# Joins and bank copies at the head of each half step of a fused FFT mixer and MLP; steps 0 and 1 side by side; table casts in stage A

## The chip, the cores and the metric

One Trainium2 chip, one core. The time is device microseconds of one launch. The kernel before has a median of 2609.62 us over 3 runs (2607.21 to 2612.15).

## The reference

For each of 8 sequences of 3008 tokens with 256 channels the reference takes a real FFT along the tokens, mixes the channels with a complex 256 x 256 matrix and a bias, applies a soft threshold of 0.01 to real and imaginary parts, and transforms back. All 24064 tokens then go through an MLP with a squared ReLU:

```python
X = np.fft.rfft(x, axis=1)
Yr = Xr @ w_r - Xi @ w_i + b_r
Yi = Xr @ w_i + Xi @ w_r + b_i
Yr = np.sign(Yr) * np.maximum(np.abs(Yr) - lam, 0.0)   # Yi likewise
y = np.fft.irfft(Y, n=x.shape[1], axis=1)
h = np.maximum(x @ w_in, 0.0)                          # w_in 256 x 2048
out = h * h @ w_out                                    # w_out 2048 x 256
```

## The kernel before

**Numbers.** Every large product is done in three matmuls (`mm3`), of a rounded high half and the low half that is left of both operands: high by high, high by low, low by high. So each tensor that TensorE (PE) reads is first split: ScalarE (ACT) casts the high half, VectorE (DVE) subtracts to get the low half.

**The transform.** 3008 = 47 x 64. Stage A transforms over 47 points, stage B over 64, then come the mix, the threshold, stage C (64 points back) and stage D (47 points back). A and B, and C and D, hand their data over through DRAM scratch. Two frequencies make a pair; there are 12 pairs for each sequence (batch). `start()` does stages A to D of batch 0 and stage A of batch 1, splits the weights that are needed first, then casts the tables of the mix (`tables_main`) and prepares the first chunk. All that uses a pool of memory of its own (`sb0`), which is given back before the main loop.

**The main loop.** The tokens are cut into 32 chunks of 752 columns. For each chunk the MLP has 8 steps (`u`), each for 256 of the 2048 hidden columns. Each step has two half steps (`r = 2u + h`, even and odd), and 516 half steps are written out in order. The first layer of a step is done with seven products (0 to 6, line 1010, a Winograd scheme over 2 x 2 blocks), three matmuls of 376 columns each. Products 0, 6, 5 and 1 add up in one PSUM bank x, which ACT copies out after each of them (lines 1127, 1142, 1157; the last with ReLU, line 1174); products 2, 4 and 3 use the other bank y, and DVE joins each to what the copies left (`join`, line 1017). The next product in a bank must wait until the copy or join of the one before it has read it. The results are squared on ACT (line 1108), split into gh (ACT, line 1113) and gl (DVE, `low`, line 1119), and two steps later (`LAG`) the second layer takes them: `mm2`, 12 matmuls in each half step, which are handed out in portions (`take_some`) between the products.

PE's order in an even half step is: product 0, product 3 of the step before, place p1, 6 of mm2, product 6, 3 of mm2, product 2, the other 3 of mm2, place p2. In an odd one: product 5, 3 of mm2, product 4, p1, 3 of mm2, product 1, the other 6 of mm2, p2.

**Transform work in the loop.** Batches 1 to 7 are transformed between the MLP's work. A planner puts each piece into a half step and a place there: `load` (DMA issues on SP, at the head), `p1` and `p2` (matmuls), `e`, `e2` and `f`, `f2` (what ACT and DVE do at once with a bank that p1 or p2 filled), and `a` (ACT) and `v` (DVE) for the rest that has no bank to empty. The rest of a pair is: xl on DVE in half step r; the threshold on DVE in r + 2; `turned` in r + 3, four ACT instructions (lines 880 and 881) that turn the thresholded halves round; zh on ACT and zl on DVE in r + 4. Stage A has fold, fh and fl there. The pairs of batch 1 stand 3 half steps apart, from r = 7 on, those of batch 2 stand 4 apart and those of batches 3 to 7 stand 5 apart (`pair_rounds`). Five tables of w_out are loaded late, one at a time into one buffer (`et`), and narrowed and split in places `a` and `v` (`plan_w`).

In the kernel before, `a` and `v` of a half step are the last thing in it. So on ACT they stand before the first bank copy of the next half step, and on DVE before `low` and, in an even half step, before join 3, which `low` precedes as well. Each engine does its instructions in the order in which they are written; waits between engines are semaphores.

The lines that the rows name: 198 to 200 are the three matmuls of `mm3`, 1025 those of mm2, 300 the low half of a chunk's operands (xa, xb, xc), 297 their high half, 856 is xl, 193 the low half of a table, 604 a copy in the first inverse, 334 the first instruction of narrowing.

Of the kernel before, what the change touches and what calls it, by code (L numbers as in the profile page):

```python
# [10 lines left out]
F32 = mybir.dt.float32  # L11
F32R = mybir.dt.float32r
U32 = mybir.dt.uint32
AF = mybir.ActivationFunctionType
ALU = mybir.AluOpType

P = 128
# [120 lines left out]
HALF = CH // 2  # L138


def crossed(x):

    return x.rearrange("p (a i) -> p i a", a=2)
# [21 lines left out]
def fft_mix_moe(ctx: ExitStack, tc: tile.TileContext, xp, xu, w_ri, b_ri,  # L165
                w_in, w_out, t_u, t_a, t_b, t_b0, t_m, t_d, sgn, outT):
    nc = tc.nc
# [22 lines left out]
    def split(src, hi, lo, engine=nc.vector):  # L190

        nc.scalar.copy(hi, src)
        engine.tensor_sub(lo, src, hi.bitcast(F32))
# [150 lines left out]
    def start():  # L344

        with ExitStack() as own:
# [82 lines left out]
            def tables_main():  # L429

                for k in range(2):
                    split(ms[:, 3 * k:3 * k + 3], wm[0][:, :, k], wm[1][:, :, k])
                    yield
                split(tM, tMs[:, 0], tMs[:, 1])
                yield
# [54 lines left out]
            def weights(begin=True):  # L490

                for p in list(going):
                    if next(p, going) is going:
                        going.remove(p)
                p = next(pending, None) if begin else None
                if p is not None:
                    next(p)
                    going.append(p)
                return bool(going)
# [89 lines left out]
            first = [i for i in range(len(flat)) if begins[i] < CH]  # L589
# [84 lines left out]
            late = table_a()  # L674
# [43 lines left out]
            inv = inverse()  # L718
            next(inv)
            nc.sync.dma_start(out=bias2.rearrange("p c e -> p (c e)"), in_=b_ri[0].partition_broadcast(P))  # L720
            for n, _ in enumerate(a1):
                for k in range(WE[n]):
                    weights()
            busy = x1[nq - 1][:NU1].rearrange("p k d -> p (k d)")
            for _ in range(WARM2):
                idle()
# [1 line left out]
                weights()  # L728
            for _ in inv:
                pass  # L730
            late = tables_main()
            while weights():
                next(late, None)
            for _ in late:
                pass

# [6 lines left out]
    ps_h = ctx.enter_context(tc.tile_pool(name="ps_h", bufs=1, space=bass.MemoryType.PSUM))  # L743
    ps_o = ctx.enter_context(tc.tile_pool(name="ps_o", bufs=1, space=bass.MemoryType.PSUM))
# [7 lines left out]
    def opnd(name, dt, bufs):  # L752
        return tl(name, (P, 2, HALF), dt, bufs=bufs)

    for tag, shape, dt, bufs in (("g0", (P, 2, HALF), F32, 2), ("g1", (P, 2, HALF), F32, 2),
                                 ("gh", (P, 2, HALF), F32R, 3), ("gl", (P, 2, HALF), F32R, 3), ("o", (P, 4, HALF), F32, 1),
                                 ("gap1", (P, 16), F32, 1), ("xh", (P, 3, 2, P), F32R, 1), ("xl", (P, 3, 2, P), F32R, 1),
                                 ("gap2", (P, 24), F32, 1), ("fh", (P, 512), F32R, 1), ("fl", (P, 512), F32R, 1),
                                 ("gap3", (P, 16), F32, 1), ("zh", (P, 2, D), F32R, 1), ("zl", (P, 2, D), F32R, 1)):
        tl(tag, shape, dt, bufs)  # L760
# [13 lines left out]
    def run(r, place):  # L774
        for do in plan.pop((r, place), ()):
            do()
# [232 lines left out]
    def product(s, u, bank, start=False):  # L1009
        c, j = divmod(u, NU)  # L1010
        name, n = XOP[s]
        w, x = wi_[j], xs_[c][name]
        mm3(bank[:, :HALF], (w[:, 0, s], w[:, 1, s]), (crossed(x[:, 0, n]), crossed(x[:, 1, n])), start, True,
            skip_group_check=True)

    def join(bank, g):
        nc.vector._custom_dve(TENSOR_ADD_SAT, out=g, in0=bank[:, :HALF], in1=g, s0=float("inf"), s1=0.0)  # L1017
# [58 lines left out]
        plan_w(j, r)  # L1076

    gs, cast, split_, pos, outs, stores = {}, {}, {}, {}, {}, []
    h0 = h1 = None

    def take_some(gen, n):
        for _ in range(n):
# [3 lines left out]
    with tc.manual_schedule():  # L1086
        for r in range(2 * (last + LAG)):
            u, h = divmod(r, 2)
            c, j = divmod(u, NU)
            k = u - LAG  # L1090
            cc, jj = divmod(k, NU)
            live, behind = u < last, 0 <= u - 1 < last
            nextx = live and c + 1 < nch and r % PER == PER - 1
            ends = k >= 0 and jj == NU - 1
            run(r, "load")
            while stores:
                stores.pop()()
            if k >= 0:
                if jj == 0:
                    pos[cc, h] = [ps_o.tile([P, 512], F32, tag=f"o{e}{h}", name="po") for e in range(2)]  # L1100
                second = mm2(jj, h, pos[cc, h], *split_.pop((k, h)))
            else:
                second = iter(())

            def squares():
                if behind:
                    g = gs[u - 1][h]
                    nc.scalar.activation(g, g, AF.Square)  # L1108

            def high():  # L1110
                if behind:
                    cast[u - 1, h] = opnd("gh", F32R, 3)
                    nc.scalar.copy(cast[u - 1, h], gs[u - 1][h])  # L1113

            def low():
                q = (u - 1, 0) if h else (u - 2, 1)
                if q in cast:
                    gh, gl = cast.pop(q), opnd("gl", F32R, 3)
                    nc.vector.tensor_sub(gl, gs[q[0]][q[1]], gh.bitcast(F32))  # L1119
                    split_[q] = gh, gl  # L1120

            if h == 0:
                if live:
                    gs[u] = [opnd(f"g{n}", F32, 2) for n in range(2)]
                    old, h0 = h1, ps_h.tile([P, 512], F32, tag="x", name="h0")
                    product(0, u, h0, True)
                    nc.scalar.copy(gs[u][0][:, 0], h0[:, :HALF])  # L1127
                else:
                    old = h1
                if behind:  # L1130
                    product(3, u - 1, old)
                low()
                if behind:
                    join(old, gs[u - 1][1][:, 0])
                run(r, "p1")
                run(r, "e")
                run(r, "e2")
                squares()
                take_some(second, 6)
                if live:  # L1140
                    product(6, u, h0)
                    nc.scalar.copy(gs[u][1][:, 0], h0[:, :HALF])  # L1142
                take_some(second, 3)
                if live:
                    h1 = ps_h.tile([P, 512], F32, tag="y", name="h1")
                    product(2, u, h1, True)
                    join(h1, gs[u][0][:, 0])
                if live and c and j == 0:
                    xc, x = new_x(c, "xc"), halves(raw_of(c))[:, 1:4:2]
                    high_x(xc, x, 0, 2)  # L1150
                    low_x(xc, x, 0, 2)
                high()
                take_some(second, 12)
            else:
                if live:
                    product(5, u, h0)
                    nc.scalar.copy(gs[u][1][:, 1], h0[:, :HALF])  # L1157
                low()
                take_some(second, 3)
                if live:  # L1160
                    product(4, u, h1, True)
                    join(h1, gs[u][1][:, 1])
                run(r, "p1")
                run(r, "e")
                run(r, "e2")
                if nextx:
                    xa, x = new_x(c + 1, "xa"), halves(raw_of(c + 1))[:, 0:3:2]
                    high_x(xa, x, 0, 2)
                    low_x(xa, x, 0, 2)
                squares()  # L1170
                take_some(second, 3)
                if live:
                    product(1, u, h0)
                    nc.scalar.activation(gs[u][0][:, 1], h0[:, :HALF], AF.Relu)
                if nextx:
                    xb = new_x(c + 1, "xb")
                    high_x(xb, ts[:, 0:3], 0, 3)
                    low_x(xb, ts[:, 0:3], 0, 3)
                high()
                take_some(second, 12)  # L1180
            run(r, "p2")
            rest = out(cc, h, pos.pop((cc, h))) if ends else iter(())
            next(rest, None)
            run(r, "f")
            run(r, "f2")
            next(rest, None)
            run(r, "a")
            run(r, "v")
            if live and c + 1 < nch and r % PER == PER - 3:
                ts = tl("o", (P, 4, HALF), name="ts")  # L1190
                diffs(c + 1, ts[:, 0:2], ts[:, 2])
        assert not stores
# [46 lines left out]
```

## Time and profile before

| | |
|---|---|
| median of 3 runs | 2609.62 us |
| the profiled execution's own time | 2608.95 us |
| its span | 2607.0 us |
| PE busy, matmuls / weight loads | 2467.1 us (95%) / 2339.3 us (90%) |
| ACT busy | 1859.0 us (71%) |
| DVE busy | 1653.1 us (63%) |
| mean granted TensorE clock | 0.993 |
| HBM traffic | 62 GB/s over the span |

The span runs from the first to the last instruction of the program. An engine's busy time is the union of its instructions' times. Matmuls overlap each other in the pipeline, so PE's busy time says less on holes than that of its weight loads (PEld), of which one stands before each matmul. In a row of the waits, the instruction on the left sat idle until the one on the right was done.

### The profile page before, as it was taken

What the parts mean: (1) busy time and instruction counts of PE and PEld (TensorE: products, weight loads), DVE (VectorE), ACT (ScalarE), POOL (GpSimd) and SP (SyncE); (2) the same over time, 40 slices, a digit from 0 to 9 for tenths busy, and PEclk for the clock granted to TensorE, in tenths of its full rate; (3) what the DMA queues carried; (4) which work ended last, traced back from release to release, by engine and by line L of the source; (5) the groups of instructions that cost most, each with busy time, mean ns of one, the idle gap of its engine ahead of it and who ended that gap; (6) DMA issues with size and microseconds to landing.
All of it is one profiled execution on the core that took longest, in us unless ns stands there. A gap on an engine that the chain in (4) does not pass through costs nothing.

```text
span 2607.0 us, 40095 instructions
## 1 busy us (share of the span) xinstructions
PE 2467.1 (95%) x15630; PEld 2339.3 (90%) x15630; DVE 1653.1 (63%) x2715; ACT 1859.0 (71%) x3332; POOL 26.1 (1%) x41
## 2 busy tenths in 40 slices
PE   9888899999999999999999999999999999999999
PEld 5478889999999889998999989998999989999999
DVE  6666666676666666666666666666666656655554
ACT  5667677777767777777777767777776767767776
POOL 2100000000000000000000000000000000000000
PEclk9999999999999999999999999999999999999999
DMA  9512132211222122121211221211211011110000
GB/s 277 163 53 78 37 98 87 75 63 44 72 60 71 55 63 68 44 75 52 66 57 56 63 67 51 73 48 59 63 61 47 26 48 42 34 43 24 24 13 25
DMA packets 107544, 164.54 MB, mean 63 GB/s; under 512 B 9065, under 2 KB 59225, under 8 KB 107354
## 3 DMA queue, kind: packets, MB, share of 16 engines
q1 hardware_dynamic: 107066, 161.59, 20.1%
q8 instruction: 123, 2.02, 0.3%
q14 instruction: 67, 0.55, 0.1%
q10 hardware_dynamic: 288, 0.39, 0.0%
HBM read 86.97 MB, written 74.97 MB: 62 GB/s over the span
## 4 chain that ended last, share of the span: by engine, by line
PE 63%; ACT 18%; DVE 11%; issue 2%; DMA 1%; DVEq 0%; ACTq 0%; SPq 0%
PE po L1025 24%; PE h L198 9%; PE h L199 8%; PE h L200 8%; DVE gl L1119 3%; ACT gh L1113 3%; PE psd L315 3%; ACT g L1108 3%; ACT z L881 2%; PE psb L243 2%; PE psm L200 2%; PE psm L199 2%; PE psm L198 2%; ACT z L880 2%; DVE g L1017 2%
## 5 line engine op out<-in xcount | busy, mean ns | idle before, releaser
L1025 PE MATMUL po<-gh,wo 128*128 128x376 f32 x4096 | 877.7, 327 | 0.0
L1017 DVE CUSTOM_DVE_ANT_0 g<-h,g 128x376 f32<-128x376 f32 x768 | 419.2, 546 | 432.6 <-PE h L200 277.2
L1025 PEld LDWEIGHTS po<-gh,wo 128*128 128x128 f32 x4096 | 681.5, 190 | 0.0
L1119 DVE TENSOR_TENSOR gl<-g,gh 128x752 fp32r<-128x752 f32 x512 | 478.5, 935 | 62.0 <-ACT gh L1113 61.2
L1025 PE MATMUL po<-gl,wo 128*128 128x376 f32 x2048 | 452.7, 323 | 0.0
L1108 ACT ACTIVATE g<-g 128x752 f32<-128x752 f32 x512 | 427.7, 835 | 1.4
L1113 ACT CAST gh<-g 128x752 fp32r<-128x752 f32 x512 | 419.1, 818 | 0.1
L1025 PEld LDWEIGHTS po<-gl,wo 128*128 128x128 f32 x2048 | 350.0, 190 | 0.0
L198 PE MATMUL h<-xb,wi 128*128 128x376 f32 x768 | 257.5, 335 | 39.1 <-ACT g L1127 38.3
L199 PE MATMUL h<-xb,wi 128*128 128x376 f32 x768 | 249.7, 325 | 0.0
L200 PE MATMUL h<-xb,wi 128*128 128x376 f32 x768 | 249.3, 325 | 0.0
L198 PE MATMUL h<-xa,wi 128*128 128x376 f32 x512 | 181.9, 355 | 63.0 <-DVE g L1017 56.4
L1157 ACT COPY g<-h 128x376 f32<-128x376 f32 x256 | 121.0, 472 | 164.4 <-PE h L200 163.5
L1142 ACT COPY g<-h 128x376 f32<-128x376 f32 x256 | 120.5, 471 | 128.1 <-DVE gl L1119 79.1
L198 PEld LDWEIGHTS h<-xb,wi 128*128 128x128 f32 x768 | 146.7, 191 | 58.4 <-ACT g L1127 54.8
L198 PE MATMUL h<-xc,wi 128*128 128x376 f32 x512 | 171.1, 334 | 21.8 <-ACT g L1157 19.0
L198 PEld LDWEIGHTS h<-xa,wi 128*128 128x128 f32 x512 | 96.9, 189 | 102.5 <-DVE g L1017 83.2
L1127 ACT COPY g<-h 128x376 f32<-128x376 f32 x256 | 121.5, 475 | 79.7 <-PE h L200 77.2
L199 PE MATMUL h<-xa,wi 128*128 128x376 f32 x512 | 167.0, 326 | 6.5 <-DVE xa L300 6.5
L200 PE MATMUL h<-xa,wi 128*128 128x376 f32 x512 | 165.9, 324 | 0.0
L199 PE MATMUL h<-xc,wi 128*128 128x376 f32 x512 | 165.4, 323 | 0.0
L200 PE MATMUL h<-xc,wi 128*128 128x376 f32 x512 | 165.3, 323 | 0.0
(138 smaller groups left out, 4193.1 us busy)
## 6 DMA issues: line engine op xcount, KB each, us to landing
bin<-s SPq DMA_DIRECT2D x96, 256.0 KB
s<-evc SPq DMA_DIRECT2D x96, 256.0 KB
outT_dram<-o SPq DMA_DIRECT2D x62, 376.0 KB
din<-s SPq DMA_DIRECT2D x96, 240.0 KB
xin<-in_xp_dram SPq DMA_DIRECT2D x72, 240.0 KB
s<-eva SPq DMA_DIRECT2D x72, 240.0 KB
s<-eva SPq DMA_DIRECT2D x38, 192.0 KB
w<-in_moe_w_in_dram SPq DMA_DIRECT2D x8, 512.0 KB
```

Source lines behind the costliest of these rows:

```text
L198: nc.tensor.matmul(out, l0, r0, start=start, stop=False, **kw)
L199: nc.tensor.matmul(out, l0, r1, start=False, stop=False, **kw)
L200: nc.tensor.matmul(out, l1, r0, start=False, stop=stop, **kw)
L315: nc.tensor.matmul(ps[:, k, part], t[:n, s:s + P], tD[:n, tab + part, :n], start=True, stop=True)
L1017: nc.vector._custom_dve(TENSOR_ADD_SAT, out=g, in0=bank[:, :HALF], in1=g, s0=float("inf"), s1=0.0)
L1025: nc.tensor.matmul(po[e][:, :HALF], wo_[j][:, k, a, e * P:e * P + P], crossed((gl if low else gh)[:, a]), start=j == 0 and not (a or k or ...
L1108: nc.scalar.activation(g, g, AF.Square)
L1113: nc.scalar.copy(cast[u - 1, h], gs[u - 1][h])
L1119: nc.vector.tensor_sub(gl, gs[q[0]][q[1]], gh.bitcast(F32))
L1127: nc.scalar.copy(gs[u][0][:, 0], h0[:, :HALF])
L1142: nc.scalar.copy(gs[u][1][:, 0], h0[:, :HALF])
L1157: nc.scalar.copy(gs[u][1][:, 1], h0[:, :HALF])
```

## The change

1. In both half steps the places `a` and `v` of half step r are now run in half step r + 1: in an even one after product 0 with its copy and product 3 with its join, ahead of `low`; in an odd one after product 5 with its copy, `low`, and product 4 with its join. In an even half step join 3 now also stands ahead of `low`. PE's order inside a half step is as it was. Only in half steps 0 and 1 do `a` and `v` still close their own half step.
2. Steps 0 and 1 are done side by side in half steps 0 and 1, one product of each in turn; step 1 uses two banks that the second layer needs only later. Half steps 2 and 3 have no first layer but product 3.
3. The tables of the mix (`tables_main`, three parts) are cast during the last eight pieces of batch 1's stage A, and no more behind the inverse.
4. g1 has three buffers instead of two.

```diff
--- before.py
+++ after.py
@@ -718,9 +718,12 @@
             inv = inverse()
             next(inv)
             nc.sync.dma_start(out=bias2.rearrange("p c e -> p (c e)"), in_=b_ri[0].partition_broadcast(P))
+            late = tables_main()
             for n, _ in enumerate(a1):
                 for k in range(WE[n]):
                     weights()
+                if n in (1, 4, 7):
+                    next(late)
             busy = x1[nq - 1][:NU1].rearrange("p k d -> p (k d)")
             for _ in range(WARM2):
                 idle()
@@ -728,9 +731,8 @@
                 weights()
             for _ in inv:
                 pass
-            late = tables_main()
             while weights():
-                next(late, None)
+                pass
             for _ in late:
                 pass
 
@@ -752,7 +754,7 @@
     def opnd(name, dt, bufs):
         return tl(name, (P, 2, HALF), dt, bufs=bufs)
 
-    for tag, shape, dt, bufs in (("g0", (P, 2, HALF), F32, 2), ("g1", (P, 2, HALF), F32, 2),
+    for tag, shape, dt, bufs in (("g0", (P, 2, HALF), F32, 2), ("g1", (P, 2, HALF), F32, 3),
                                  ("gh", (P, 2, HALF), F32R, 3), ("gl", (P, 2, HALF), F32R, 3), ("o", (P, 4, HALF), F32, 1),
                                  ("gap1", (P, 16), F32, 1), ("xh", (P, 3, 2, P), F32R, 1), ("xl", (P, 3, 2, P), F32R, 1),
                                  ("gap2", (P, 24), F32, 1), ("fh", (P, 512), F32R, 1), ("fl", (P, 512), F32R, 1),
@@ -1076,7 +1078,7 @@
         plan_w(j, r)
 
     gs, cast, split_, pos, outs, stores = {}, {}, {}, {}, {}, []
-    h0 = h1 = None
+    banks = {}
 
     def take_some(gen, n):
         for _ in range(n):
@@ -1119,32 +1121,65 @@
                     nc.vector.tensor_sub(gl, gs[q[0]][q[1]], gh.bitcast(F32))
                     split_[q] = gh, gl
 
-            if h == 0:
-                if live:
-                    gs[u] = [opnd(f"g{n}", F32, 2) for n in range(2)]
-                    old, h0 = h1, ps_h.tile([P, 512], F32, tag="x", name="h0")
-                    product(0, u, h0, True)
-                    nc.scalar.copy(gs[u][0][:, 0], h0[:, :HALF])
+            def first():
+                gs[u] = [opnd(f"g{n}", F32, 2 + n) for n in range(2)]
+                banks[u] = [ps_o.tile([P, 512], F32, tag=f"o{n}1", name="h0") if u == 1 else
+                            ps_h.tile([P, 512], F32, tag="xy"[n], name="h0") for n in range(2)]
+
+            def snap(s, u, n, a, start=False):
+                product(s, u, banks[u][0], start)
+                nc.scalar.copy(gs[u][n][:, a], banks[u][0][:, :HALF])
+
+            def joined(s, u, n, a, start=False):
+                product(s, u, banks[u][1], start)
+                join(banks[u][1], gs[u][n][:, a])
+
+            def fourth(u):
+                product(1, u, banks[u][0])
+                nc.scalar.activation(gs[u][0][:, 1], banks[u][0][:, :HALF], AF.Relu)
+
+            if u == 0:
+                if h == 0:
+                    for u in range(2):
+                        first()
+                        snap(0, u, 0, 0, True)
+                    for u in range(2):
+                        joined(2, u, 0, 0, True)
+                    for u in range(2):
+                        snap(6, u, 1, 0)
+                    run(r, "p1")
+                    run(r, "e")
+                    run(r, "e2")
                 else:
-                    old = h1
+                    for u in range(2):
+                        snap(5, u, 1, 1)
+                    for u in range(2):
+                        joined(4, u, 1, 1, True)
+                    run(r, "p1")
+                    run(r, "e")
+                    run(r, "e2")
+                    for u in range(2):
+                        fourth(u)
+                u = 0
+            elif h == 0:
+                if live and u > 1:
+                    first()
+                    snap(0, u, 0, 0, True)
                 if behind:
-                    product(3, u - 1, old)
+                    joined(3, u - 1, 1, 0)
+                run(r - 1, "a")
+                run(r - 1, "v")
                 low()
-                if behind:
-                    join(old, gs[u - 1][1][:, 0])
                 run(r, "p1")
                 run(r, "e")
                 run(r, "e2")
                 squares()
                 take_some(second, 6)
-                if live:
-                    product(6, u, h0)
-                    nc.scalar.copy(gs[u][1][:, 0], h0[:, :HALF])
+                if live and u > 1:
+                    snap(6, u, 1, 0)
                 take_some(second, 3)
-                if live:
-                    h1 = ps_h.tile([P, 512], F32, tag="y", name="h1")
-                    product(2, u, h1, True)
-                    join(h1, gs[u][0][:, 0])
+                if live and u > 1:
+                    joined(2, u, 0, 0, True)
                 if live and c and j == 0:
                     xc, x = new_x(c, "xc"), halves(raw_of(c))[:, 1:4:2]
                     high_x(xc, x, 0, 2)
@@ -1152,14 +1187,14 @@
                 high()
                 take_some(second, 12)
             else:
-                if live:
-                    product(5, u, h0)
-                    nc.scalar.copy(gs[u][1][:, 1], h0[:, :HALF])
+                if live and u > 1:
+                    snap(5, u, 1, 1)
                 low()
                 take_some(second, 3)
-                if live:
-                    product(4, u, h1, True)
-                    join(h1, gs[u][1][:, 1])
+                if live and u > 1:
+                    joined(4, u, 1, 1, True)
+                run(r - 1, "a")
+                run(r - 1, "v")
                 run(r, "p1")
                 run(r, "e")
                 run(r, "e2")
@@ -1169,9 +1204,8 @@
                     low_x(xa, x, 0, 2)
                 squares()
                 take_some(second, 3)
-                if live:
-                    product(1, u, h0)
-                    nc.scalar.activation(gs[u][0][:, 1], h0[:, :HALF], AF.Relu)
+                if live and u > 1:
+                    fourth(u)
                 if nextx:
                     xb = new_x(c + 1, "xb")
                     high_x(xb, ts[:, 0:3], 0, 3)
@@ -1184,8 +1218,9 @@
             run(r, "f")
             run(r, "f2")
             next(rest, None)
-            run(r, "a")
-            run(r, "v")
+            if u == 0:
+                run(r, "a")
+                run(r, "v")
             if live and c + 1 < nch and r % PER == PER - 3:
                 ts = tl("o", (P, 4, HALF), name="ts")
                 diffs(c + 1, ts[:, 0:2], ts[:, 2])
```

## Rows read from the trace of the kernel before

**Rows 1.** The page, part 1: busy us (share of the span) and instructions
```profile
PE 2467.1 (95%) x15630; PEld 2339.3 (90%) x15630; DVE 1653.1 (63%) x2715; ACT 1859.0 (71%) x3332; POOL 26.1 (1%) x41
```

**Rows 2.** Busy time by window, without transform work: engines' us, PEclk, DMA, GB/s
```profile
2500.00:2560.00 60.00, 59.75 (x374) 59.27 (x373) 33.15 (x51) 43.05 (x73) 0.00 (x0) 1.00 0.04 14
```

**Rows 3.** Waits of the weight loads after 200 us: total us, times, longest
```profile
PEld h L198 <- DVE g L1017: 78.5, 89, 2.9
PEld h L198 <- ACT g L1127: 46.1, 56, 3.3
PEld h L198 <- ACT g L1157: 28.3, 40, 2.5
PEld h L198 <- ACT g L1174: 13.2, 38, 0.9
PEld h L199 <- DVE xa L300: 8.7, 9, 1.2
```

**Rows 4.** The chain that ended last, 500 to 520 us: start, us, what
```profile
511.89 0.96 PE po L1025 x6
```

**Rows 5.** Timeline: a product behind a join; start, us, instruction, idle before
```profile
711.51 0.19 PEld L198 LDWEIGHTS h<-xc,wi 128*128 128x128 f32 x1
...
713.54 0.96 DVE L856 TENSOR_TENSOR xl<-x,xh 128x768 fp32r<-128x768 f32 x1
...
714.41 0.93 DVE L1119 TENSOR_TENSOR gl<-g,gh 128x752 fp32r<-128x752 f32 x1
...
715.27 0.54 DVE L1017 CUSTOM_DVE_ANT_0 g<-h,g 128x376 f32<-128x376 f32 x1
...
715.86 0.19 PEld L198 LDWEIGHTS h<-xa,wi 128*128 128x128 f32 x1 [1.00 <-DVE g L1017]
```

**Rows 6.** Timeline: even half step with `turned` before it
```profile
802.01 0.19 PEld L198 LDWEIGHTS h<-xa,wi 128*128 128x128 f32 x1
...
802.50 0.41 ACT L880 COPY z<-et 64x256 f32<-64x256 f32 x1
...
804.38 0.47 ACT L1127 COPY g<-h 128x376 f32<-128x376 f32 x1
...
804.91 0.19 PEld L198 LDWEIGHTS h<-xb,wi 128*128 128x128 f32 x1 [0.96 <-ACT g L1127]
...
805.69 0.47 ACT L1142 COPY g<-h 128x376 f32<-128x376 f32 x1
...
806.77 0.19 PEld L198 LDWEIGHTS h<-xb,wi 128*128 128x128 f32 x1
```

**Rows 7.** Timeline: odd half step with `turned` before it
```profile
828.18 0.19 PEld L198 LDWEIGHTS h<-xb,wi 128*128 128x128 f32 x1
828.19 0.41 ACT L880 COPY z<-et 64x256 f32<-64x256 f32 x1
...
830.07 0.47 ACT L1157 COPY g<-h 128x376 f32<-128x376 f32 x1
...
830.59 0.19 PEld L198 LDWEIGHTS h<-xc,wi 128*128 128x128 f32 x1 [0.47 <-ACT g L1157]
...
831.98 0.19 PEld L198 LDWEIGHTS h<-xa,wi 128*128 128x128 f32 x1
```

**Rows 8.** Waits of ACT after 200 us
```profile
ACT g L1142 <- DVE gl L1119: 74.2, 80, 2.9
```

**Rows 9.** Timeline from the inverse to step 2
```profile
112.41 0.36 ACT L604 COPY dv<-psd 128x240 f32<-128x240 f32 x1 [4.31 <-PE psd L315]
...
123.39 1.82 DVE L193 TENSOR_TENSOR wm<-wmf,wm 128x768 fp32r<-128x768 f32 x2
...
125.49 0.47 ACT L1127 COPY g<-h 128x376 f32<-128x376 f32 x1 [1.45 <-issue]
...
143.15 0.67 ACT L334 ACTIVATE z<-et 128x512 f32<-128x512 f32 x1 [3.09 <-DMA et<-in_moe_w_out_dram]
...
147.56 0.19 PEld L198 LDWEIGHTS h<-xa,wi 128*128 128x128 f32 x1 [1.87 <-DVE g L1017]
```

## The prediction

> **What bounds the kernel now.** I read the page first, then a late stretch without transform work, then the waits of the weight loads, then the timeline around three of those waits. The page has TensorE busy for 95% of the span and its weight loads for 90% [rows 1]. Matmuls overlap, so the weight loads show better what is left: about 10%. Where no transform work is mixed in, loads fill 59.27 of 60 us [rows 2]. So the MLP alone runs without holes, and the holes come from the transform sharing ScalarE (ACT) and VectorE (DVE) with the bank copies and joins. After 200 us nearly all holes stand before the first matmul of a product: 78.5 us behind a join, 46.1, 28.3 and 13.2 us behind the copies of products 0, 5 and 1, and 8.7 us behind the low half of xa [rows 3], 174.8 us together. A matmul of 376 columns takes a slot of 0.96/6 = 0.16 us [rows 4]; all sums below are in such slots. TensorE's order inside a half step stays as it is, so a gain can only come from these five rows and from the start.
>
> **The joins (DVE).** Of these holes, most is product 2, which starts in the bank that join 3 empties. In [rows 5] product 3 begins at 711.51, but its join comes at 715.27, behind a cast rest (xl, 0.96) and low (gl, 0.93); product 2 is loaded at 715.86, held 1.00 us. In the changed order xl and gl follow the join, which takes 0.54. Between the end of product 3 and product 2 TensorE has 6+3+3 = 12 slots, 1.9 us, and any product of place p1 on top; the join and its hand-off need some 0.7. So the hole closes unless DVE itself is late, as at the end of a chunk, where the casts of xb and the differences still stand ahead. I leave 5 of the 78.5 us; bounds 0 and 25 (one hole of 0.8 at each of 31 chunk ends). What is late next on DVE: the rest and low now run after product 3 has ended, and join 2, which product 4 needs, is behind both. From product 0's end: 0.48 for product 3, 0.1, join 0.54, rest 0.96, low 0.93, join 2 0.54, together 3.6 us, where product 4 is due after 27 slots, 4.3 us. That hides it; if the rest must wait for its ACT cast, which now also comes later, a few of them show: 3 us, bounds 0 and 20. In odd half steps join 4 already had slack (its row is too small to stand in the waits), and putting the rest behind it gives nothing.
>
> **The bank copies (ACT).** Here I expect no gain, and this is the choice that decides the number. Putting a copy ahead of the casts frees its bank early, but ACT can then not start the casts while the product still runs; they stand between this copy and the next one, and the next bank comes late instead. The heavy case is `turned`, four instructions, 802.50 to 804.38 = 1.88 us [rows 6]; there are 7 x 12 = 84 of them.
> Even half step [rows 6]: the work from the first `turned` to the end of copy 6 is 3.66 us (802.50 to 805.69 + 0.47). Before, product 6 was held 0.96. After, ACT starts with copy 0 when product 0 is there, 802.01 plus an estimated five slots = 802.8, and ends copy 6 at 806.5. Product 5, loaded at 806.77 after that hold, would unheld be due at 805.81: held 0.7. Gain 0.3.
> Odd half step [rows 7]: product 5 is there at 828.18 + 0.8 = 829.0. ACT needs turned 1.88, copy and squares 1.31 as in the even one, relu like a copy 0.47, together 3.66, and is done at 832.65. Product 0 was loaded at 831.98 after a hold of 0.47, so is due at 831.51: held 1.15. Loss 0.7, because before, ACT had begun `turned` at 828.19, while product 5 ran.
> By the code 48 of the 84 fall in even and 36 in odd half steps (the pairs of batch 2 stand 4 apart, all even; the others alternate). A product in p1 or p2 lengthens TensorE's part and hides the hold. At that distance from its pair only groups of stages A (78) and D (100 in the loop) can stand there, 178 in 512 half steps, so about 0.35 to 0.4 are covered, which leaves about 0.3 in an even and 0.8 in an odd one (p1 also brings a copy of its bank to ACT). Even: 48 x (0.6 x 0.7 + 0.4 x 0.3) = 26; odd: 36 x (0.6 x 1.15 + 0.4 x 0.8) = 36. The same shares on the holds of before give 48 x (0.6 x 0.96 + 0.4 x 0.3) = 33 and 36 x 0.6 = 22 (odd ones with and without ACT's lead lie between 0.47 and 0.9), 55 of the 87.6 us of the three copies; the other 32 come from casts shorter than 0.7 us, copies of transform banks and chunk ends. Some of these profit, I keep 28. After: 26 + 36 + 28 = 90, against 87.6: +2. Bounds: -60 (the two earlier copies' 74.4 us go, less 14 that stays on relu) and +60 (no cover, and ACT's delay passed on to the next half step in half of the cases).
> The third buffer of g1 belongs here: copy 6 waits 74.2 us for low to read the old one [rows 8]. Before, product 5 had time for that. Now low ends later, so with two buffers this wait would reach TensorE; with three it is gone. No term of its own.
> The low half of xa at a chunk end waits for its ACT cast, which in the new order comes behind the odd half step's rest: 8.7 becomes 12, +3; bounds -3 and +12.
>
> What the order of a queue does is seen in [rows 6]: copy 0 starts at 804.38, after four casts, though product 0 was loaded at 802.01; nothing passed the casts. The Trainium skill (PSUM — Partial Sum Buffer, Engine vs sequencer instructions) says that the queues of ScalarE and VectorE are strictly first in, first out; it speaks against the change, since a copy that waits then holds all casts behind it. The trace agrees. By that rule the ACT term is +2; were casts free to pass a waiting copy, ACT would keep its lead in both kinds of half step, the term would be about -45, and the time 2493.
>
> **Start: tables and steps 0 and 1.** Mix's tables are cast after the inverse; their last DVE piece runs 123.39 to 125.21 (a small one of tM follows), and the first bank copy starts at 125.49 [rows 9]. In the change these casts stand among stage A's copies, before ACT's 4.31 us of idle time that ends at 112.41, so about 2 us of ACT and DVE work are hidden there; uncovered they would cost 2. The first copy moves up by 2 to 3 us, to the end of the xc casts. Steps 0 and 1 side by side fill holes of a stretch whose pace is set by the three loads of late w_out tables: each is needed by ACT in order, the third one at 143.15 after 3.09 us of waiting, and behind it are copy 0 of step 2, low, join 3 and product 2 at 147.56 [rows 9]. The loads follow the first one, so they move with it. Copy 0 and join 3 now stand ahead of the third table, but copy 6, low and join 2 do not. I take -5; bounds -9 and 0. The load issues keep their places at the head of a half step; a load of et waits as before for narrowing of the one before, now half a step later, with SP's later loads behind it. A half step lasts (2607 - 125)/516 = 4.8 us and the transform's loads are issued two to four half steps ahead, so I count that at 0, at worst +3.
>
> **Sum.** The profiled execution took 2608.95 us (span 2607.0 and 1.95 around it), 0.67 below the median of the runs, 2609.62. -78.5 + 5 + 3 + 2 + 3 - 5 = -70.5, so 2538.5; on the median's scale 2539. I say 2538.
>
> **Rivals.**
> 1. Both engines' holes close. The copies profit as the joins do: the -60 of ACT comes in. For it: ACT is busy for only 71% [rows 1]. Against: the two worked half steps, where the work between two copies exceeds TensorE's time whatever the average is. Time 2539 - 62 = 2477.
> 2. The joins' gain is half given back: product 4 held by join 2 (+20), ACT without cover (+20). Time about 2580.
> 3. The join's wait is not one of order: it stays where DVE is late for other reasons, and only the start gains. For it: DVE waits for ACT casts too. Against: in [rows 5] the two instructions ahead of the join are just the ones that move. Time 2604 to 2609.
> 4. Slower: ACT late for good. Place: the rest behind a waiting copy in an odd half step delays relu, then gh, then the next copy 0, so that a `turned` costs 1.2 at product 0 and another 0.7 at the next product 5. 84 x 1.9 + 28 = 188 against 87.6, +100, with 70 gained: 2638. It decides where the half step after a `turned` gives ACT less than about 0.5 us back. Against: that half step has only zh of its pair, a third of `turned` as an estimate by its size, and an even half step without `turned` has 1.88 - 0.7 = 1.2 us to spare by [rows 6].
>
> **How the numbers follow.** Forecast (2505 to 2570) 0.60, rival 1 0.15, rival 2 0.13, rival 3 0.05, rival 4 0.07. The range cuts half of rival 1 and rivals 3 and 4: 2490 to 2590. Within 0.2% (5 us) of the time before, about what a measurement of this kernel can tell from no change: 0.04, from rival 3. Slower 0.07, faster 0.89.
>
> **What would show it.** Right, step by step: the hold by joins falls from 78.5 to under 15 us; the holds by copies 0 and 5 shrink to under 10 each, while product 0 (behind relu) grows from 13.2 to some 45 and a new one, product 5 behind copy 6, stands at 25 to 35; the first bank copy starts by 123.6. Wrong: if the sum of the four ACT holds is under 45, rival 1 holds; if products 3 or 4 show holds behind joins over 20 us, rival 2; if product 2 is still held for over 40, rival 3. A product 0 held over 90 us would be rival 4.

## The result and the profile after

The changed kernel takes 2500.19 us (median of 4 runs, 2499.42 to 2500.79) against 2608.43 us of before: ratio 0.9583, 95% interval 0.9566 to 0.9599. The profiled execution took 2499.91 us, 109.0 less than the one of before, with a span of 2498.0. On the page after, part 1, TensorE's weight loads now fill 93% of the span, by the same work:

```profile
span 2498.0 us, 39815 instructions
...
PE 2429.7 (97%) x15630; PEld 2333.2 (93%) x15630; DVE 1655.2 (66%) x2715; ACT 1856.0 (74%) x3332; POOL 26.1 (1%) x41
```

The waits of the weight loads after 200 us (us in total, times, longest). Line 1019 is the join (1017 before), 1131 the copy of products 0, 6 and 5 (1127, 1142, 1157), 1139 relu of product 1 (1174):

```profile
PEld h L198 <- ACT g L1139: 47.7, 68, 2.1
PEld h L198 <- ACT g L1131: 28.1, 60, 1.6
PEld h L199 <- DVE xa L300: 5.9, 9, 0.9
PEld h L198 <- DVE g L1019: 1.1, 3, 0.4
```

Against [rows 3]: joins 78.5 to 1.1, the three ACT rows 87.6 to 75.8, xa 8.7 to 5.9. Line 1131 stands for three products. By operand of the waiting load (xb: products 6, 5 and, behind joins, 4; xc: 1 and 3; busy us, mean ns, idle before) it is this:

```profile
L198 PEld LDWEIGHTS h<-xb,wi 128*128 128x128 f32 x744 | 140.6, 189 | 29.6 <-ACT g L1131 27.0 <-DVE g L1019 1.1
...
L198 PEld LDWEIGHTS h<-xc,wi 128*128 128x128 f32 x497 | 93.9, 189 | 1.1 <-ACT g L1131 1.1
```

So product 1 is held no more (1.1), and of xb's 27.0 I count in the timeline 21 before product 5, where there was nothing, and 6 before product 6. Product 0, behind relu, went from 13.2 to 47.7. ACT's holds moved to the next bank, as forecast. The even and the odd half step with `turned` behind the copy, which answer to [rows 6] and [rows 7]:

```profile
766.78 0.19 PEld L198 LDWEIGHTS h<-xa,wi 128*128 128x128 f32 x1
...
767.62 0.47 ACT L1131 COPY g<-h 128x376 f32<-128x376 f32 x1 [0.23 <-PE h L200]
...
767.99 0.40 ACT L882 COPY z<-et 64x256 f32<-64x256 f32 x1
...
768.69 0.19 PEld L198 LDWEIGHTS h<-xb,wi 128*128 128x128 f32 x1
...
769.87 0.83 ACT L1110 ACTIVATE g<-g 128x752 f32<-128x752 f32 x1
...
770.61 0.45 ACT L1131 COPY g<-h 128x376 f32<-128x376 f32 x1
...
771.11 0.19 PEld L198 LDWEIGHTS h<-xb,wi 128*128 128x128 f32 x1 [0.48 <-ACT g L1131]
...
790.90 0.19 PEld L198 LDWEIGHTS h<-xb,wi 128*128 128x128 f32 x1
...
791.74 0.47 ACT L1131 COPY g<-h 128x376 f32<-128x376 f32 x1 [0.72 <-PE h L200]
...
792.11 0.40 ACT L882 COPY z<-et 64x256 f32<-64x256 f32 x1
...
792.81 0.19 PEld L198 LDWEIGHTS h<-xc,wi 128*128 128x128 f32 x1
...
793.97 0.83 ACT L1110 ACTIVATE g<-g 128x752 f32<-128x752 f32 x1
794.71 0.47 ACT L1139 ACTIVATE g<-h 128x376 f32<-128x376 f32 x1
...
795.23 0.19 PEld L198 LDWEIGHTS h<-xa,wi 128*128 128x128 f32 x1 [0.95 <-ACT g L1139]
```

Even: copy 0 at 767.62, then `turned`, square, copy 6 at 770.61, and product 5 held 0.48 (0.7 forecast). Odd: copy 5 at 791.74, `turned`, square, relu at 794.71, and product 0 held 0.95 (1.15 forecast).

The start (timeline): the first two copies now stand at 121.77, where the first copy stood at 125.49 [rows 9], and the first table of w_out is asked for at 121.83. But ACT still waits 3.00 us for the third table, and product 5 of step 2 behind it 4.19 us:

```profile
121.77 0.85 ACT L1131 COPY g<-h 128x376 f32<-128x376 f32 x2 [0.33 <-issue]
121.83 0.39 SPq L1052 DMA_DIRECT2D et<-in_moe_w_out_dram  x1
...
139.59 0.66 ACT L334 ACTIVATE z<-et 128x512 f32<-128x512 f32 x1 [3.00 <-DMA et<-in_moe_w_out_dram]
...
141.65 0.29 PEld L198 LDWEIGHTS h<-xb,wi 128*128 128x128 f32 x1 [4.19 <-ACT g L1131]
```

### The profile page after: what moved, and what is told of

Read it like the earlier page. It is cut to its first block, busy times and chain, and to the rows that moved or that the text cites. A ratio compares the mean times of both kernels' runs of the same rounds, so it can differ in the third digit from the quotient of the medians.

```text
span 2498.0 us, 39815 instructions
## 1 busy us (share of the span) xinstructions
PE 2429.7 (97%) x15630; PEld 2333.2 (93%) x15630; DVE 1655.2 (66%) x2715; ACT 1856.0 (74%) x3332; POOL 26.1 (1%) x41
## 4 chain that ended last, share of the span: by engine, by line
PE 82%; ACT 13%; DVE 2%; DMA 2%; issue 1%; SPq 0%; ACTq 0%; DVEq 0%
PE po L1027 32%; PE h L198 11%; PE h L199 10%; PE h L200 10%; PE psd L315 3%; PE psb L243 3%; ACT z L883 3%; ACT g L1110 3%; PE psm L198 3%; PE psm L200 3%; PE psm L199 3%; ACT z L882 2%; ACT g L1131 2%; ACT g L1139 1%; PE psa L519 1%
## 5 line engine op out<-in xcount | busy, mean ns | idle before, releaser
L198 PE MATMUL h<-xa,wi 128*128 128x376 f32 x512 | 173.2, 338 | 32.8 <-ACT g L1139 32.0
L198 PEld LDWEIGHTS h<-xb,wi 128*128 128x128 f32 x768 | 145.8, 190 | 42.2 <-ACT g L1131 37.7
L199 PE MATMUL h<-xa,wi 128*128 128x376 f32 x512 | 166.5, 325 | 4.1 <-DVE xa L300 4.1
L198 PE MATMUL h<-xc,wi 128*128 128x376 f32 x512 | 166.1, 324 | 1.4 <-DVE g L1019 1.2
L199 PE MATMUL h<-xc,wi 128*128 128x376 f32 x512 | 165.3, 323 | 0.0
L200 PE MATMUL h<-xa,wi 128*128 128x376 f32 x512 | 165.3, 323 | 0.0
L200 PE MATMUL h<-xc,wi 128*128 128x376 f32 x512 | 165.3, 323 | 0.0
L198 PE MATMUL psm<-wm,xh 128*128 128x256 f32 (+1 forms) x552 | 157.8, 286 | 0.7 <-ACT xh L550 0.7
L200 PE MATMUL psm<-wm,xl 128*128 128x256 f32 (+1 forms) x552 | 157.2, 285 | 0.9 <-DVE xl L551 0.8
L199 PE MATMUL psm<-wm,xh 128*128 128x256 f32 (+1 forms) x552 | 156.8, 284 | 0.0
```

The source lines that it names most:

```text
L198: nc.tensor.matmul(out, l0, r0, start=start, stop=False, **kw)
L199: nc.tensor.matmul(out, l0, r1, start=False, stop=False, **kw)
L200: nc.tensor.matmul(out, l1, r0, start=False, stop=stop, **kw)
```

## The experiments

The time of the changed kernel stands at 2500.2 throughout; ratios are against the kernel before on the same chip.

**1. The casts back ahead of the copies, joins stay first.**

```diff
-            if u == 0:
+            if u == 0 or r >= 8:
                 run(r, "a")
+            if u == 0:
                 run(r, "v")
```

> The changed kernel with ACT's rest (place a) back at the end of its own half step from half step 8 on, so ahead of the next bank copy; DVE's rest stays behind the joins. Theory (the joins are the gain; the copies only move ACT's holds from products 6 and 1 to products 5 and 0, and are worth little): holds before products 0 and 5 fall under 25 us together, those before products 6 and 1 come back to 70 to 100, join holds stay under 10; 2505 to 2530 us. Rival (the copies at the head are the larger part, the joins follow from them): 2560 us or more. Rival (copies and casts can change places at no cost at all): 2497 to 2503 us with the holds unchanged in sum.

2519.06 us, ratio 0.9658 (0.9644 to 0.9673). Waits of the weight loads after 200 us:

```profile
PEld h L198 <- ACT g L1131: 78.1, 100, 3.3
PEld h L198 <- ACT g L1139: 13.2, 38, 0.9
```

Joins hold nothing, and ACT holds 91.3 us where the kernel before had 87.6, so with the joins' holes gone ACT loses hardly any lead. By product they stand where they stood before: 46.8 us before product 6, 31.2 before 1, 13.2 before 0 and none before 5. The order on DVE with the changed start (and g1's third buffer, which was not tried without the copies at the head) makes 90 of the 109 us; the copies at the head add 18.9. The theory holds with its range; against the prediction, which had the copies cost 2 us, their worth was missed.

**2. The rest and low back ahead of the joins, copies stay first.**

```diff
-                if behind:
-                    joined(3, u - 1, 1, 0)
                 run(r - 1, "a")
                 run(r - 1, "v")
+                if behind:
+                    product(3, u - 1, banks[u - 1][1])
                 low()
+                if behind:
+                    join(banks[u - 1][1], gs[u - 1][1][:, 0])
```

(In odd half steps `a` and `v` likewise stand behind product 5's copy and ahead of low.)

> The changed kernel with DVE's rest and low back ahead of the joins; the bank copies stay at the head. Theory (order on DVE made the hold of product 2): the hold behind joins comes back from 1 us to 60 to 90, the holds behind ACT fall a little, since ACT catches up in them; 2555 to 2585 us. Rival (join 3 was late because ACT was late): join holds stay under 30 us, 2500 to 2530 us.

2617.93 us, ratio 1.0033 (1.0020 to 1.0047): a little slower than before, and well past the theory's upper end. The waits of its weight loads from 200 to 2500 us:

```profile
PEld h L198 <- DVE g L1019: 107.6, 107, 3.5
PEld h L198 <- ACT g L1139: 47.7, 67, 2.1
PEld h L198 <- ACT g L1131: 22.3, 53, 1.4
```

The longest wait of its DVE for ACT after 200 us:

```profile
DVE zl L891 <- ACT zh L887: 175.0, 83, 4.3
```

The same wait in the kernel before:

```profile
DVE zl L889 <- ACT zh L885: 77.2, 53, 2.8
```

The join holes come back, and larger: 107.6. DVE's rest must wait for its ACT cast (zl for zh: 175.0 us, 77.2 before), the cast now starts only behind a bank copy, and low and the join queue behind that wait. So the copies at the head are worth 19 us with the joins ahead of the rest; without that the kernel is 9 us slower than before, even with the changed start. About half of the loss stands in the start: product 0 of step 7 comes at 200.4 us, at 195.1 before, because the stretch from the first bank copy to it takes 75.5 us instead of 69.6. The two halves of the change are not independent; my forecast had one sentence and 3 us for that.

**3. The square behind the second bank copy, in every half step.**

```diff
-                squares()
                 take_some(second, 6)
                 if live and u > 1:
                     snap(6, u, 1, 0)
+                squares()
```

(Odd: behind relu and xb.)

> The changed kernel with the squaring moved behind the second bank copy of a half step (behind copy 6, and behind relu of product 1 and the xb casts). Theory (the 76 us that are left behind ACT are the work between two copies, turned 1.9 + squares 0.8 against TensorE's 1.9 to 3.5 us): the square leaves that stretch, the holds before products 0 and 5 fall to 15 to 35 us together, those before 6 and 1 rise to 5 to 20; 2445 to 2475 us. Rival (ACT is late by its total load, so the holds only move to products 6 and 1): sum of ACT holds 65 us or more, 2490 to 2505 us.

2508.69 us, ratio 0.9618 (0.9602 to 0.9634): the rival was right on the holds, though the time lies above its range too. By operand of the waiting load (xb: 6 and 5, xc: 1, xa: 0):

```profile
L198 PEld LDWEIGHTS h<-xb,wi 128*128 128x128 f32 x744 | 140.5, 189 | 47.8 <-ACT g L1131 41.7 <-DVE g L1019 3.9
...
L198 PEld LDWEIGHTS h<-xc,wi 128*128 128x128 f32 x497 | 93.8, 189 | 17.0 <-ACT g L1131 16.6
...
L198 PEld LDWEIGHTS h<-xa,wi 128*128 128x128 f32 x496 | 93.7, 189 | 20.3 <-ACT g L1139 18.2
```

And of its waits:

```profile
PEld h L199 <- DVE xa L300: 9.4, 15, 0.9
```

Product 0 falls from 47.7 to 18.2, but product 1 rises from 1.1 to 16.6 and xb from 27.0 to 41.7: 76.5 in sum, against 75.8 in the changed kernel. Most of the 8.5 us stands on DVE's side: the holds behind joins grow from 1.1 to 3.9 us, those behind xa from 5.9 to 9.4. Sorted by half step, ACT's holds fall from 59.5 to 31.8 us where `turned` stands, and grow from 16.3 to 44.7 elsewhere. So in a half step without `turned` the stretch between the first and the second copy had room, the one behind the second copy (gh, the copies of transform banks, and now the square) had not.

**4. Two buffers of g1.**

```diff
-                gs[u] = [opnd(f"g{n}", F32, 2 + n) for n in range(2)]
+                gs[u] = [opnd(f"g{n}", F32, 2) for n in range(2)]
```

(The list of buffers at the head of the loop has 2 for g1 as well.)

> The changed kernel with two buffers of g1, as before. Theory (low now ends later, and copy 6 waits for it): a new wait of ACT for gl of 100 us or more, of which 20 to 50 us reach product 5; 2520 to 2550 us. Rival (as in the kernel before, none of this wait reaches TensorE): 2498 to 2504 us.

2527.35 us, ratio 0.9690 (0.9676 to 0.9705). ACT's wait for gl from 200 to 2500 us:

```profile
ACT g L1131 <- DVE gl L1121: 117.4, 138, 2.1
```

And the hold behind the copies, in the waits of its weight loads:

```profile
PEld h L198 <- ACT g L1131: 50.6, 100, 2.6
```

Copy 6 waits 117.4 us for low, and the hold behind line 1131 grows from 28.1 to 50.6. The third buffer is worth 27 us, though in the kernel before, with the same wait of 74.2 us [rows 8], no weight load waited for copy 6 (line 1142).

**5 and 6. Only where `turned` stands: the square late, or `turned` in two halves.**

```diff
+                if r - 1 not in turns:
+                    squares()
                 take_some(second, 6)
                 if live and u > 1:
                     snap(6, u, 1, 0)
+                if r - 1 in turns:
+                    squares()
```

(`turns` holds the half steps in which the planner puts a `turned`, r + 3 of each pair. In odd half steps the square moves behind relu likewise.)

> The changed kernel; only in the 84 half steps that carry a turned (1.9 us) the square stands behind the second bank copy, elsewhere it stays. Theory (a hold is the work between two neighbouring copies; moving the square in every half step helped the 84 and hurt the others, whose second stretch was full already): product 0's hold falls from 45.6 to 20 to 30 us, product 5's from 20 to about 10, products 6 and 1 rise by 5 to 15 together; 2470 to 2488 us. Rival (what is taken out of one stretch comes back in the next one, turned or not): sum of ACT holds stays at 70 to 80, 2495 to 2506 us.

```diff
-        at(r + 3, "a", turned)
+        at(r + 3, "a", lambda: turned(0))
+        at(r + 3, "a2", lambda: turned(1))
...
                     snap(6, u, 1, 0)
+                run(r - 1, "a2")
```

(`turned(q)` does the two instructions of one frequency of the pair. In odd half steps `a2` stands behind relu.)

> The changed kernel with turned in two halves of 0.95 us: the first pair of instructions behind the first bank copy, the second pair behind the second one. Theory (work between two copies): product 0's hold falls from 45.6 to 15 to 25 us, product 5's from 20 to 5 to 10, products 6 and 1 rise by 5 to 10 together; 2465 to 2482 us. Rival (load over the whole half step decides): sum of ACT holds 70 us or more, 2495 us or more.

2464.69 us (0.9448, 0.9434 to 0.9461) and 2457.96 us (0.9425, 0.9411 to 0.9439). The second is the fastest version found, 1.7% under the changed kernel. Waits of the weight loads in experiment 5 (lines 1140 and 1132 are relu and the copy):

```profile
PEld h L198 <- ACT g L1140: 25.1, 64, 1.3
PEld h L198 <- ACT g L1132: 13.2, 31, 1.4
```

The same in experiment 6 (lines 1142 and 1134):

```profile
PEld h L198 <- ACT g L1142: 19.6, 52, 1.1
PEld h L198 <- ACT g L1134: 13.5, 31, 1.4
```

The four ACT holds fall from 75.8 to 38.3 and to 33.1 us, and the time by 35.5 and 42.2. In the half steps with `turned` they fall from 59.5 to 15.0 and to 8.5 us, in the others they grow from 16.3 to 23.2 and to 24.6. So most of what is left to hold in the changed kernel is `turned` together with the square between two neighbouring copies; taking a part of it to the next stretch, in those 84 half steps alone, keeps the gain that experiment 3 undid elsewhere. Both came out a little better than expected.

**7. Mix's tables behind the inverse again.**

```diff
-            late = tables_main()
...
-                if n in (1, 4, 7):
-                    next(late)
...
+            late = tables_main()
             while weights():
-                pass
+                next(late, None)
```

> The changed kernel with the mix's tables cast behind the inverse again. Theory: ACT's 1.9 us come back ahead of the first bank copy, the loads of w_out tables start about 2 us later, and the start is 1 to 3 us longer: 2501 to 2503 us. Rival (the start is set by the chain of five loads, which waits for nothing that the tables hold): within 0.7 us of the changed kernel.

2502.53 us, ratio 0.9594 (0.9580 to 0.9608).

**8. Steps 0 and 1 one behind the other** (the general branch for every step, banks x and y for step 1 too).

```diff
-            if u == 0:
+            if False:
...
-                if live and u > 1:
+                if live:
```

> The changed kernel with steps 0 and 1 one behind the other again, all else as changed. Theory (the pace of the start is set by the late tables' loads, steps side by side only move idle time of TensorE): 0 to 3 us longer, 2500 to 2503 us. Rival (the holes of steps 0 and 1 were the start's cost): 5 us or more longer.

2501.49 us, ratio 0.9592 (0.9578 to 0.9607). Both intervals overlap that of the changed kernel, so by these times neither part of the start can be told from nothing; the 18.9, 8.5 and 27 us of experiments 1, 3 and 4 can. The timelines can tell. The last copy of the inverse in the changed kernel (its first bank copy, at 121.77, is shown above):

```profile
115.22 0.36 ACT L604 COPY dv<-psd 128x240 f32<-128x240 f32 x1 [1.14 <-PE psd L315]
```

The same copy and the first bank copy in experiment 7:

```profile
117.92 0.36 ACT L604 COPY dv<-psd 128x240 f32<-128x240 f32 x1 [0.91 <-PE psd L315]
...
127.26 0.85 ACT L1129 COPY g<-h 128x376 f32<-128x376 f32 x2 [1.46 <-issue]
```

From one to the other it takes 6.55 us in the changed kernel, 9.34 in experiment 7 and 9.33 in the kernel before (116.16 to 125.49): the tables are worth 2.8 us. From the first bank copy to product 0 of step 7 it takes 69.5 us in the changed kernel, 69.8 in experiment 8 and 69.6 before: steps side by side are worth next to nothing. Both theories hold. The last copy of the inverse itself came between 115.2 and 118.3 us in profiles of kernels that are alike up to there (the changed kernel, experiments 2, 4 and 8), which hides a part of this size in the times.

## Why the prediction was right, and where its sizes were off

The time lies in the range (2490 to 2590), but 5 us below the band that was given to the forecast itself (2505 to 2570). By its mechanism that is the case that came: join holes closed, ACT's holds for the most part moved rather than removed. The gain was forecast too small, 70.5 against 109.0 us, and all terms but the start missed to the same side; the range held by its width:

| term | forecast | measured |
|---|---|---|
| joins, with product 4 behind join 2 | -78.5 + 5 + 3 = -70.5 | -77.4 |
| bank copies | +2 | -11.8 |
| low half of xa | +3 | -2.8 |
| start, to product 0 of step 7 (195.3 to 191.5 in the timeline) | -5 | -3.8 |
| rest | 0 | -13.2 |

**Joins.** The argument by slots held: with the join ahead, product 2's hole is gone, at the chunk ends too, where I had kept 5 us. After 200 us joins hold 1.1 us in all, before product 4.

**Bank copies.** The step that failed is the term +2. Its two worked cases were right. Sorting the holds after 200 us by half step (product 5 goes with the even half step whose copy 6 was late, product 0 with the odd one whose relu was), I count 22.6 us in the even ones with `turned` (26 forecast; 36.0 before) and 36.9 in the odd ones (36; 24.5 before). What was mis-sized is the remainder without `turned`: 28 us were kept, 16.3 are left of 27.2. A cast of 0.6 us ahead of a copy held product 6 or 1; behind it, it fits into the room that the other stretch has: in these half steps products 6 and 1 were held 17.8 us before and are held 5.3 after, product 0 9.4 and 10.9. Experiment 1, which puts ACT's casts back, has 17.8 and 9.4 again. It prices the copies at the head at 18.9 us, and its 91.3 us of ACT holds also show that what ACT loses of its lead when the join holes close is worth 4 us. Of the signs, product 5 came out lower than said, 21 us against 25 to 35.

**xa.** The sign was wrong, by 6 us. It goes with the order on DVE: with the casts back (experiment 1) the row is much the same, 6.6, with the rest and low back ahead of the joins (experiment 2) it is 10.6.

**Rest.** This is the largest thing that the sum left out: it had no term for TensorE's clock. In the kernel before, the granted clock stood at 1.2 GHz in seven stretches between 200 us and the end of the loop, each within 1.4 us behind a hold of 2.2 us or more; the largest hold of the changed kernel after 200 us is 2.1 us, and its clock does not fall again until the end of the program. Two of those holds, in the timeline of before:

```profile
311.97 0.22 PEld L198 LDWEIGHTS h<-xb,wi 128*128 128x128 f32 x1 [3.31 <-ACT g L1127]
...
2137.15 0.19 PEld L198 LDWEIGHTS h<-xa,wi 128*128 128x128 f32 x1 [2.92 <-DVE g L1017]
```

The stretch behind each, and the first 300 us of the loop, in the table of busy time by stretch, also of before (sum, then PE, PEld, DVE, ACT, POOL, the granted clock, DMA share and GB/s):

```profile
312.20:315.40 3.20, 3.20 (x11) 3.20 (x11) 0.17 (x1) 2.68 (x5) 0.00 (x0) 0.50 0.08 20
2138.30:2141.50 3.20, 3.20 (x11) 2.93 (x10) 1.13 (x2) 1.41 (x3) 0.00 (x0) 0.50 0.07 26
200.00:500.00 300.00, 277.05 (x1792) 266.63 (x1791) 195.72 (x330) 215.10 (x388) 0.00 (x0) 0.98 0.25 74
```

The first 300 us of the loop in the changed kernel:

```profile
200.00:500.00 300.00, 287.63 (x1929) 279.75 (x1928) 208.23 (x352) 227.70 (x415) 0.00 (x0) 1.00 0.25 79
```

Seven stretches of 3.4 us at half the clock cost some 7 x 3.4 / 2 = 12 of the 13 us. That the clock fell because of the holds is argued from the order in time and not shown. No run here sets it apart; two holds of 2.2 us in the kernel before (at 867 and 1505 us) had no such stretch behind them; of the seven holds of 2.2 us or more in experiments 1, 2 and 4 only three had one; and in experiment 2 the clock also fell behind shorter holds (one of 2.1 us, and 1.4 and 1.0 us in a row). The mean clock of the kernel before also differs from execution to execution, from 0.991 to 0.995, so this term is that of one pair of profiles.

**Start.** The size was right, with the tables as nearly all of it. The first copy came 3.7 us earlier: 2.8 by the tables (experiment 7), 0.9 ahead of them, where executions differ by more than that. Steps side by side gave next to nothing (experiment 8). ACT's work on the third table, at 139.59 instead of 143.15, kept nearly all of the 3.7; but product 5 of step 2 is then held 4.19 us behind that table, as forecast.

**Rivals.** Rival 1 (ACT's 60 us go too) is out: the four holds are 75.8 us, not under 45. Only experiments 5 and 6 go below its 2477 us. Rival 2 is out (joins hold 1.1 us), rival 3 too. Rival 4 had a mechanism that exists, in experiment 2: the copies at the head made the kernel slower than before, but through DVE's waits for late casts, not through relu. (The 2493 beside these, for casts that could pass a waiting copy, is a slip: -45 in place of the +2 gives 2492.)

## What to carry to other kernels

On engines that work in program order, put what frees a bank ahead of what only has to be done some time; then look at what now stands between two neighbouring releases, because the hold moves there. Add up that stretch against TensorE's work in the same stretch, and split or move only the piece that overfills it: moving 0.8 us in every half step lost 8.5 us, moving it in one half step of six gained 35.5. When the order on one engine changes, do it on the engine that waits for its results as well.

## What the runs showed of the hardware that was not expected

A hold of TensorE of 2.2 to 3.5 us inside a loop that is otherwise full was followed by 3.4 us at 1.2 GHz in seven of nine cases of the kernel before, and in three of seven in experiments 1, 2 and 4. Holds of the same length went either way: 2.25 us, ended at 1184.86 in the kernel before, was followed by such a stretch, and 2.25 us, ended at 1504.76, was not. Such a stretch costs some 1.7 us beyond the hold itself, if the hold is the cause (not tested here). The price of a hold is therefore better read from the clock's column as well as from the waits.
